# Linear attention, soft mixture of experts and an x − tanh(x) layer in one program: M is split into two parts while it is 128 columns wide, and the order of the last stage changes

## The chip, the cores and the metric

The program runs on one core of a Trainium2 chip. A core has TensorE (PE; its weight loads are shown apart, as PEld), VectorE (DVE), ScalarE (ACT), GpSimd (POOL) and SyncE (SP, which here only issues transfers). Each takes its instructions in a fixed order, written into the program beforehand. The metric is the device time of one execution in microseconds (us).

## What is computed

Three stages follow one another; the change is in the last, and in what hands over to it.

```python
# 1. attention with decay, in blocks: attn[4, 8, 768, 64] -> x[3072, 512]
# 2. soft mixture of experts
logits = x @ phi                                   # phi [512, 32]
d = softmax over tokens;  slot_input = d.T @ x     # 32 slots
h = np.maximum(slot_input[e] @ w1[e], 0.0)         # 8 experts
slot_out[e] = h @ w2[e]                            # [32, 512]
c = softmax(logits over the 32 slots)              # [3072, 32]
x = c @ slot_out
# 3. second layer, w_in [512, 2048], w_out [2048, 512]
h = x @ w_in
g = h - np.tanh(h)
out = g @ w_out
```

## The kernel before

**The last stage.** Since x = c @ slot_out, the product x @ w_in is c @ M with M = slot_out @ w_in, a matrix of only 32 rows and 2048 columns. The kernel never forms x: it makes M, and then h, 128 of its columns by 512 tokens at a time. For small h, h − tanh(h) is close to h³/3, and the kernel computes it as a mean part and a product: with d the deviation from the mean, r = (d + a) · (d²/3), where a comes from a table; what this leaves over is linear in c and is added at the end (the linear part, 32 columns wide). A check at the end of the program chooses a slower exact path, which these inputs do not take.

**Numbers in two parts.** A full-precision (fp32) product shows as two records on PE; a product of operands in the rounded form (fp32r) shows as one. To keep precision with rounded products, c stands in four slices of 32 rows of `c4` (rounded, rest, rounded, mean), and M stands in `ms` [128 rows, 2048 columns]: rows 0 to 63 the rounded M twice, rows 64 to 95 its rest.

**Chunks and turns.** The work is 96 chunks, numbered n. Chunk n is a pair (c, f): 512 tokens c and 128 columns f of h. `TURNS` lists the order: turns of 2, 2, 2, 4, 8, 12, 10 chunks and so on, each of one c; in the early turns only few f are there, since the weights still arrive. For a chunk, `d_of` forms d in one of three PSUM banks (0 to 2; L805), `s_of` squares it on ScalarE (L809), `r_of` multiplies on VectorE (L823; for seven chunks in `POOL_R` on GpSimd, L821), and `product` makes four products of 512 columns into banks 3 to 6 (L830, called t = 0 to 3 below). At a turn's end `keep` adds the four banks to `part` (ScalarE copies them when the turn begins at f = 0, L836; otherwise VectorE adds, L838), and the next turn reuses the banks. d runs three chunks ahead (`LA`), except for the chunks in `LATE`. In the last step of a turn the products of its last two chunks stand together, bank by bank.

**Weights.** w_in and w_out arrive as 64-bit numbers in slabs (`wi0`, `wo0`, `wi1`, ...), each by two transfers into a ring of three buffers, so that a slab's transfer waits until an earlier slab is used up. A slab is turned to fp32 by two `cast` steps on GpSimd (L117) and two `join` steps on VectorE (L121); `round_wo` rounds w_out (ScalarE L788, GpSimd L790). `DECODE_AT` and `LEAD` say at which chunk each step stands.

**M.** When two slabs of w_in are there, `make_m` forms 512 columns of M folded to 128 (four bands of 32 rows; L753, one PSUM bank called `MISC`), and a copy brings them to SBUF (L758). `put_m` spreads them out to `ms` through PSUM with the 0/1 matrix `put` (L765); ScalarE writes all 128 rows, rounding (L769), and VectorE then overwrites rows 64 to 95 with the difference (L770). `turn_m` makes a transposed copy for the table `mt` (L778, L781). The first 512 columns (m = 0) go in two halves, named (0, 0) and (0, 1) below; `HALF` and `DUE` say at which chunk. d of a chunk with f needs its columns of `ms`.

**The order** is written out by hand: a loop over n in which each call stands where its instructions go on every engine's queue, with `at(n, f)` for what is appended to step n:

```python
        if n + LA < NN and n + LA not in LATE:
            ahead()
        if n + LA - 1 < NN:
            r_of(n + LA - 1)
```

Matrix products on unused data (`keep_warm`, numbers in `WARM_MAIN`) stand in some waits.

## Time and profile before

| what | us |
|---|---|
| median of 3 runs (from 311.28 to 312.46) | 311.6 |
| the profiled execution, its own time | 311.51 |
| its span, from first to last instruction | 309.6 |
| PE busy, of the span | 294.8 |
| DVE busy | 181.3 |
| ACT busy | 134.3 |
| POOL busy | 115.2 |

The span is what the trace shows; 1.9 us lie around it. Times below are from the span's start. The last stage begins at about 155 us. The granted clock of TensorE is 0.995 of full speed over the span. Of two records in a row on PE the distance between starts counts, since products are pipelined: the length of one record holds the way through the array too.

### The profile page before, as it was taken

What the parts mean: (1) busy time and instruction counts of PE and PEld (TensorE: products, weight loads), DVE (VectorE), ACT (ScalarE), POOL (GpSimd) and SP (SyncE); (2) the same over time, 40 slices, a digit from 0 to 9 for tenths busy, and PEclk for the clock granted to TensorE, in tenths of its full rate; (3) what the DMA queues carried; (4) which work ended last, traced back from release to release, by engine and by line L of the source; (5) the groups of instructions that cost most, each with busy time, mean ns of one, the idle gap of its engine ahead of it and who ended that gap; (6) DMA issues with size and microseconds to landing.
All of it is one profiled execution on the core that took longest, in us unless ns stands there. A gap on an engine that the chain in (4) does not pass through costs nothing.

```text
span 309.6 us, 7420 instructions
## 1 busy us (share of the span) xinstructions
PE 294.8 (95%) x2996; PEld 213.6 (69%) x2996; DVE 181.3 (59%) x330; ACT 134.3 (43%) x280; POOL 115.2 (37%) x167
## 2 busy tenths in 40 slices
PE   8999999999999999999989889999999899999992
PEld 7788787878878774445466567777655677787771
DVE  4844455544654244520269667696872877968783
ACT  1433343344333433232248669586633554454420
POOL 6366566765653104112276445686600001000000
PEclk9999999999999999999999999999999999999997
DMA  6999999999999999999988747562000030303154
GB/s 209 386 402 395 396 399 394 395 399 398 392 403 396 383 362 344 389 393 396 391 308 318 268 142 285 194 230 110 0 2 0 2 135 0 135 2 135 70 202 143
DMA packets 32679, 79.77 MB, mean 258 GB/s; under 512 B 3008, under 2 KB 3328, under 8 KB 32640
## 3 DMA queue, kind: packets, MB, share of 16 engines
q1 hardware_dynamic: 32512, 79.18, 68.5%
q8 instruction: 25, 0.41, 0.5%
q14 instruction: 14, 0.11, 0.1%
q0 software_dynamic: 128, 0.07, 0.1%
HBM read 72.94 MB, written 6.29 MB: 256 GB/s over the span
## 4 chain that ended last, share of the span: by engine, by line
PE 80%; DVE 8%; issue 4%; DMA 3%; ACT 2%; POOL 1%; DVEq 0%; ACTq 0%; POOLq 0%
PE ops L830 22%; PE sc L286 7%; PE xp L310 7%; PE dps L805 6%; PE op L610 5%; PE hp L586 5%; PE xnp L344 4%; PE xp L303 4%; DVE r L823 3%; PE up L319 3%; DMA qk<-in_qkv 3%; DVE part L838 2%; PE ltp L333 2%; PE ap L388 2%; PE wp L419 2%
## 5 line engine op out<-in xcount | busy, mean ns | idle before, releaser
L830 PE MATMUL ops<-wr,r 128*128 128x512 f32 (+1 forms) x388 | 109.0, 397 | 1.2 <-ACT part L836 0.9
L830 PEld LDWEIGHTS ops<-wr,r 128*128 128x128 f32 x388 | 72.3, 188 | 22.2 <-ACT part L836 3.1
L809 ACT ACTIVATE s<-dps 128x512 f32<-128x512 f32 x96 | 56.9, 603 | 54.1 <-PE dps L805 52.8
L823 DVE SCALAR_TENSOR_TENSOR r<-dps,mt,s 128x512 fp32r<-128x512 f32 x89 | 64.8, 746 | 20.2 <-ACT s L809 19.4
L805 PE MATMUL dps<-c,ms 128*128 128x512 f32 x96 | 39.5, 425 | 4.2 <-DVE r L823 2.3
L290 DVE TENSOR_TENSOR at<-sc,dtab 128x512 f32<-128x512 f32 x48 | 30.8, 683 | 15.1 <-PE sc L286 15.1
L265 POOL TENSOR_TENSOR kc<-k,dtab 128x512 f32<-128x512 f32 x20 | 21.2, 1058 | 26.6 <-PE up L319 23.6
L258 POOL TENSOR_TENSOR qs<-qk,ql 128x512 f32<-128x512 f32 x20 | 25.5, 1275 | 14.6 <-DMA qk<-in_qkv 14.5
L346 ACT COPY xn<-xnp 128x512 f32<-128x512 f32 x24 | 14.0, 585 | 38.9 <-PE xnp L344 38.9
L286 PE MATMUL sc<-qk 64*128 64x128 f32 x384 | 27.9, 285 | 1.4 <-DMA qk<-in_qkv 1.4
L805 PEld LDWEIGHTS dps<-c,ms 128*128 128x128 f32 x96 | 17.9, 188 | 15.6 <-DVE r L823 7.8
L310 PE MATMUL xp<-at,v 128*64 128x128 f32 x384 | 26.3, 279 | 0.0
L286 PEld LDWEIGHTS sc<-qk 64*128 64x128 f32 x384 | 23.3, 187 | 4.2 <-issue 1.9
L313 ACT COPY xt<-xp 128x256 f32<-128x256 f32 x48 | 17.9, 372 | 16.9 <-PE xp L310 16.4
L310 PEld LDWEIGHTS xp<-at,v 128*64 128x64 f32 x384 | 20.5, 136 | 4.1 <-issue 3.9
L325 DVE TENSOR_TENSOR st<-up,sd 128x256 f32<-128x256 f32 x16 | 6.8, 425 | 23.4 <-PE up L319 22.0
L117 POOL CAST top<-wi 128x512 f16<-128x512 bf16 x16 | 14.3, 907 | 13.7 <-DMA wi<-in_w_in 13.1
L838 DVE TENSOR_TENSOR part<-ops,part 128x512 f32<-128x512 f32 (+1 forms) x29 | 17.9, 665 | 0.9 <-PE ops L1066 0.9
L610 PE MATMUL op<-w,hz 128*32 128x512 f32 x128 | 16.5, 594 | 0.0
L117 POOL CAST top<-wo 128x512 f16<-128x512 bf16 x16 | 15.2, 978 | 2.3 <-DMA wo<-in_w_out 2.1
L121 DVE SCALAR_TENSOR_TENSOR wif<-wi,top 128x512 uint32<-128x512 uint32 x16 | 13.3, 842 | 4.2 <-POOL top L117 4.2
L344 PE MATMUL xnp<-cst,xt 128*128 128x128 f32 x96 | 15.7, 287 | 0.0
(185 smaller groups left out, 344.3 us busy)
## 6 DMA issues: line engine op xcount, KB each, us to landing
w<-in_w SPq DMA_DIRECT2D x64, 512.0 KB, 8.4
qk<-in_qkv SPq DMA_DIRECT2D x24, 512.0 KB, 8.4
wi<-in_w_in SPq DMA_DIRECT2D x16, 512.0 KB, 4.0
wo<-in_w_out SPq DMA_DIRECT2D x16, 512.0 KB, 4.2
v<-in_qkv SPq DMA_DIRECT2D x24, 256.0 KB, 8.5
...
```

The lines of the kernel that those rows point to most:

```text
L117: nc.gpsimd.tensor_copy(out=every(top().bitcast(F16), 2, 1)[:, sl], in_=every(raw().bitcast(BF16)[:, 4:], 4, 0)[:, sl])
L258: nc.gpsimd.tensor_tensor(out=qs_t[u], in0=qk_t[u][:, 0], in1=ql, op=ALU.mult)
L286: nc.tensor.matmul(sc[h2][:, p], qk[sl, 1, p], qk[sl, 0, p], start=True, stop=True)
L290: nc.vector.tensor_tensor(out=by_head(at_t[u], h2), in0=sc[h2], in1=by_head(dtab, h2), op=ALU.mult)
L310: nc.tensor.matmul(at_head(p, h2), v[:, h * DH:(h + 1) * DH], at[:, h], start=c == 0 and p < 2, stop=True, skip_group_check=True)
L344: nc.tensor.transpose(xnp[:, p], xt[:, p // 2, p % 2], ident)
L610: nc.tensor.matmul(op[g * NS:(g + 1) * NS], hz_t[e % 3][:, q], w2_t[e, q // 4][:, g], start=e == 0 and q < 4, stop=e == NE - 1 and q >= 4, ...
L805: nc.tensor.matmul(d_t[n], ms[:, f * P:(f + 1) * P], c4[:, c], start=True, stop=True)
L809: nc.scalar.activation(out=s, in_=d_t[n], func=AF.Square, scale=math.sqrt(1.0 / 3))
L823: nc.vector.scalar_tensor_tensor(out=r_t[n], in0=d, scalar=mt[:, f, NS:], in1=s, op0=ALU.add, op1=ALU.mult)
L830: nc.tensor.matmul(op, r_t[n][:, t * P:(t + 1) * P], wr_t[f // 2][:, f % 2, sl], start=first, stop=last)
L838: nc.vector.tensor_tensor(out=pt, in0=op, in1=pt, op=ALU.add)
```

## The change

It makes six edits, all in what builds the instruction order.

1. `make_m` no longer only copies M: ScalarE writes the rounded M (`mh`) and VectorE the rest (`ml`), while M is 128 columns wide. `put_m` and `turn_m` use two rounded products each, one for `mh` and one for `ml`; `put` is 192 columns wide, so that `ml` lands on rows 64 to 95. The VectorE step on `ms` goes.
2. s and r of chunk 0 are made in two halves of 256 columns, and the products of chunk 0 stand ahead of d of chunk 3.
3. The two joins of `wi1`, which stood behind r of chunk 1, stand behind r of chunk 2 and of chunk 3.
4. The halves of m = 0 and the set m = 1 get places of their own (`HALF`, `SECOND`): `make_m(0, 1)` and `put_m(1)` stand in the middle of a turn's last products (`at_mid`), and `split` and `take` among the keeps. For all sets `put_m` now stands ahead of `turn_m`.
5. s of chunk 8 (`LATE`) stands behind the keeps of its step.
6. The linear part's end: one ScalarE copy, one VectorE difference and a ScalarE copy of 16 rows, in place of two ScalarE copies and four VectorE steps. The table `ends` goes. Two products of `keep_warm` go, one from each of two waits.

```diff
-WARM_MAIN = 2, 1, 2, 3, 1
+WARM_MAIN = 2, 1, 1, 2, 1
-HALF = 2, 3, 4
+HALF = 3, 4, 5
+SECOND = 7, 9, 9
...
+    mh, ml = (main.tile([P, P], F32R, name=n) for n in ("mh", "ml"))
...
-        m_t[m] = lt_all[:, DM + m % 2 * P:DM + (m % 2 + 1) * P]
-        (nc.vector.tensor_copy if half == 1 else nc.scalar.copy)(m_t[m][rows], mp_[rows])
+        def split():
+            nc.scalar.activation(out=mh[rows], in_=mp_[rows], func=AF.Copy)
+            nc.vector.tensor_tensor(
+                out=ml[rows], in0=mp_[rows], in1=mh[rows].bitcast(F32), op=ALU.subtract)
+        return split
...
         for j in js:
-            nc.tensor.matmul(
-                pp[:, j], put[rows, j], m_t[m][rows], start=True, stop=True, skip_group_check=True)
-        nc.scalar.activation(out=ms[:, sl], in_=pp, func=AF.Copy)
-        nc.vector.tensor_tensor(
-            out=ms[64:96, sl], in0=pp[64:96], in1=ms[64:96, sl].bitcast(F32), op=ALU.subtract)
+            for i, t in enumerate((mh, ml)):
+                nc.tensor.matmul(
+                    pp[:, j], put[rows, j, i * 64:i * 64 + P], t[rows], start=i == 0, stop=i == 1, skip_group_check=True)
+        def take():
+            nc.scalar.activation(
+                out=ms[:, m * 512 + js[0] * P:m * 512 + (js[-1] + 1) * P],
+                in_=pp[:, js[0]:js[-1] + 1].rearrange("p j f -> p (j f)"), func=AF.Copy)
...
-        nc.tensor.matmul(
-            tp.rearrange("p j s -> p (j s)"), m_t[m][rows],
-            tsel[rows, js[0]:js[-1] + 1].rearrange("p j s -> p (j s)"), start=True, stop=True)
+        for i, t in enumerate((mh, ml)):
+            nc.tensor.matmul(
+                tp.rearrange("p j s -> p (j s)"), t[rows],
+                tsel[rows, js[0]:js[-1] + 1].rearrange("p j s -> p (j s)"), start=i == 0, stop=i == 1)
...
+    pieces = lambda n: [slice(512)] if n else [slice(256), slice(256, 512)]
...
-            lambda: nc.vector.tensor_tensor(out=ql[96:], in0=qr[96:], in1=qh[96:], op=ALU.subtract),
-            lambda: nc.vector.tensor_scalar(
-                out=ql[96:], in0=ql[96:], scalar1=ends[96:, 1:2], scalar2=0.0, op0=ALU.mult, op1=ALU.add),
-            lambda: nc.vector.scalar_tensor_tensor(
-                out=qc[96:], in0=qh[96:], scalar=ends[96:, 0:1], in1=ql[96:], op0=ALU.mult, op1=ALU.add),
+            lambda: nc.scalar.activation(out=qc, in_=qr, func=AF.Copy),
             lambda: nc.vector.tensor_tensor(
-                out=qc[64:96], in0=qr[64:96], in1=qh[64:96], op=ALU.subtract),
+                out=qc[lo], in0=qr[lo], in1=qc[lo].bitcast(F32), op=ALU.subtract),
+            lambda: nc.scalar.activation(out=qc[96:112], in_=qr[96:112], func=AF.Copy),
...
-    now(early[1:])
+    cast_1, join_0, join_1, *early = early[1:]
+    now([cast_1] + early)
+    at_r(0, join_0)
+    at_r(1, join_1)
...
         if w == "wi" and i == 1:
-            at(HALF[0], lambda: make_m(0, 1))
-            at(HALF[1], lambda: turn_m(0, 1))
-            at(HALF[2], lambda: put_m(0, 1))
+            at_mid(HALF[0], lambda: make_m(0, 1))
+            at(HALF[1], lambda: put_m(0, 1)())
+            at(HALF[2], lambda: turn_m(0, 1))
+        elif w == "wi" and i == 3:
+            at(SECOND[0], lambda: make_m(1)())
+            at_mid(SECOND[1], lambda: put_m(1))
+            at(SECOND[2], lambda: turn_m(1))
         elif w == "wi" and i % 2:
-            at(n + DUE[0], lambda: make_m(i // 2))
-            at(n + DUE[1], lambda: turn_m(i // 2))
-            at(n + DUE[2], lambda: put_m(i // 2))
+            at(n + DUE[0], lambda: make_m(i // 2)())
+            at(n + DUE[1], lambda: put_m(i // 2)())
+            at(n + DUE[2], lambda: turn_m(i // 2))
...
-        if not last and (f + 2 != hi or n == 0):
+        if 0 < n and f + 2 < hi:
             for s in ops:
                 product(*s, n, f == lo, False)
         if last:
-            for s in ops:
+            take = None
+            for i, s in enumerate(ops):
+                if i == 2:
+                    take = run(n, due_mid)
...
             if n + LA in LATE:
-                ahead()
-            for s in ops:
+                d_of(n + LA)
+            for i, s in enumerate(ops):
+                if i == 2 and take:
+                    take()
                 keep(c, *s, lo, hi)
+            if n + LA in LATE:
+                s_of(n + LA)
```

**Where instructions stand, first place.** On PE, from the placing of the half (0, 0) of M to the products of the first turn, before (`pp` is put_m's, `tp` turn_m's, `wp` keep_warm's, `dps` d's, `ops` the products of a chunk, `mp` make_m's):

```order
L765 MATMUL pp<-lt_all,put 128x128 x2
L778 MATMUL tp<-tsel,lt_all 128x66
L624 MATMUL wp<-c_1932 128x512 x2
L805 MATMUL dps<-c_1932,ms 128x512 x3
L624 MATMUL wp<-c_1932 128x512 x3
L805 MATMUL dps<-c_1932,ms 128x512
L830 MATMUL ops<-wr_2332,r 128x512 x4
L805 MATMUL dps<-c_1932,ms 128x512
L830 MATMUL ops<-wr_2332,r 128x512 x4
L805 MATMUL dps<-c_1932,ms 128x512
L753 MATMUL mp__2509<-wif_2321,so 32x128 x8
```

and the same place on PE now:

```order
L776 MATMUL pp<-mh,put 128x128
L776 MATMUL pp<-ml,put 128x128
...
L791 MATMUL tp<-tsel,ml 128x66
L625 MATMUL wp<-c_1932 128x512
L818 MATMUL dps<-c_1932,ms 128x512 x3
L625 MATMUL wp<-c_1932 128x512 x2
L848 MATMUL ops<-wr_2336,r 128x512 x4
L818 MATMUL dps<-c_1932,ms 128x512 x2
L848 MATMUL ops<-wr_2336,r 128x512 x4
L818 MATMUL dps<-c_1932,ms 128x512 x2
L848 MATMUL ops<-wr_2336,r 128x512 x4
L760 MATMUL mp__2529<-wif_2325,so 32x128 x8
```

The four products of chunk 0 have moved ahead of d of chunk 3, and make_m of the half (0, 1) has moved from ahead of d of chunk 6 to the middle of the next turn's products.

**Second place.** On PE, from the end of make_m of the set m = 1 to d of chunk 14, before (turn 3 ends in the row `x8`):

```order
L753 MATMUL mp__2619<-wif_2321,so 32x128 x2
L805 MATMUL dps<-c_1932,ms 128x512
L830 MATMUL ops<-wr_2333,r 128x512 x8
L778 MATMUL tp<-tsel,lt_all 128x132
L805 MATMUL dps<-c_1932,ms 128x512
L830 MATMUL ops<-wr_2332,r 128x512 x4
L765 MATMUL pp<-lt_all,put 128x128 x4
L805 MATMUL dps<-c_1932,ms 128x512
```

and now:

```order
L760 MATMUL mp__2623<-wif_2325,so 32x128 x2
L818 MATMUL dps<-c_1932,ms 128x512 x2
L848 MATMUL ops<-wr_2337,r 128x512 x4
L776 MATMUL pp<-mh,put 128x128
L776 MATMUL pp<-ml,put 128x128
...
L848 MATMUL ops<-wr_2337,r 128x512 x4
L791 MATMUL tp<-tsel,mh 128x132
L791 MATMUL tp<-tsel,ml 128x132
L818 MATMUL dps<-c_1932,ms 128x512
L848 MATMUL ops<-wr_2336,r 128x512 x4
L818 MATMUL dps<-c_1932,ms 128x512
```

put_m has moved from directly ahead of d of chunk 14 to the middle of the last products of turn 3, ahead of d of chunk 13; and make_m stands one chunk earlier, ahead of the d of chunk 11 that it stood behind.

**Third place.** On DVE, the linear part's end among the r's (`e`, `qc`) and the keeps behind it (`part`), before:

```order
L823 SCALAR_TENSOR_TENSOR r<-dps,mt,s 128x512 x6
L897 TENSOR_TENSOR e<-qr,lt_all 32x512
L823 SCALAR_TENSOR_TENSOR r<-dps,mt,s 128x512
L898 TENSOR_SCALAR e<-e,ends 32x512
L823 SCALAR_TENSOR_TENSOR r<-dps,mt,s 128x512
L900 SCALAR_TENSOR_TENSOR qc<-lt_all,ends,e 32x512
L823 SCALAR_TENSOR_TENSOR r<-dps,mt,s 128x512
L902 TENSOR_TENSOR qc<-qr,lt_all 32x512
L823 SCALAR_TENSOR_TENSOR r<-dps,mt,s 128x512 x2
L838 TENSOR_TENSOR part_2343<-ops,part_2343 128x512 x4
```

and now:

```order
L888 TENSOR_TENSOR lt_all<-lt_all,g_2405 128x512
L840 SCALAR_TENSOR_TENSOR r<-dps,mt,s 128x512 x6
L913 TENSOR_TENSOR qc<-qr,qc 64x512
L840 SCALAR_TENSOR_TENSOR r<-dps,mt,s 128x512 x5
L856 TENSOR_TENSOR part_2347<-ops,part_2347 128x512 x4
```

Three of the four extra steps between the r's have gone from this queue.

## Rows read from the trace of the kernel before

**Rows 1.** The page: shares of the chain that ended last, by engine

```profile
PE 80%; DVE 8%; issue 4%; DMA 3%; ACT 2%; POOL 1%; DVEq 0%; ACTq 0%; POOLq 0%
```

**Rows 2.** Windows: stretch, its us, busy us per engine (instructions), PEclk, DMA

```profile
176.00:190.00 14.00, 12.53 (x82) 9.88 (x75) 9.66 (x17) 10.20 (x20) 6.74 (x8) 1.00 0.61 212
...
250.00:262.00 12.00, 12.00 (x55) 9.09 (x54) 8.43 (x18) 6.13 (x11) 1.05 (x5) 1.00 0.12 44
```

**Rows 3.** Timeline (start, us, engine, line): d of two neighbouring chunks, undisturbed

```profile
251.09 0.40 PE L805 MATMUL dps<-c,ms 128*128 128x512 f32 x1
...
252.26 0.39 PE L805 MATMUL dps<-c,ms 128*128 128x512 f32 x1
```

**Rows 4.** Timeline: the half (0, 0) of M, to the first r

```profile
156.38 0.26 ACT L758 COPY lt_all<-mp__2403 64x128 f32<-64x128 f32 x1 [1.17 <-PE mp__2403 L753]
...
156.69 0.71 PE L765 MATMUL pp<-lt_all,put 64*128 64x128 f32 x4 [0.36 <-ACT lt_all L758]
...
157.44 0.38 ACT L769 ACTIVATE ms<-pp 128x256 fp32r<-128x256 f32 x1 [0.80 <-PE pp L765]
...
157.85 0.42 DVE L770 TENSOR_TENSOR ms<-pp,ms 32x256 fp32r<-32x256 f32 x1 [1.99 <-ACT ms L769]
...
158.33 0.97 PE L805 MATMUL dps<-c,ms 128*128 128x512 f32 x3
...
158.87 1.57 ACT L809 ACTIVATE s<-dps 128x512 f32<-128x512 f32 x3 [1.04 <-PE dps L805]
...
159.50 1.41 DVE L823 SCALAR_TENSOR_TENSOR r<-dps,mt,s 128x512 fp32r<-128x512 f32 x2 [0.24 <-ACT s L809]
...
160.64 1.10 PE L830 MATMUL ops<-wr,r 128*128 128x512 f32 x4
```

**Rows 5.** Timeline: turns 0 to 3, joins, keeps, products and make_m

```profile
160.82 2.11 DVE L121 SCALAR_TENSOR_TENSOR wif<-wi,top 128x512 uint32<-128x512 uint32 x2
...
162.51 2.05 ACT L836 COPY part<-ops 128x512 f32<-128x512 f32 x4
...
164.17 0.68 DVE L121 SCALAR_TENSOR_TENSOR wf<-wo,top 128x512 uint32<-128x512 uint32 x1
...
165.41 2.02 PE L830 MATMUL ops<-wr,r 128*128 128x512 f32 x8
...
172.36 1.97 PE L830 MATMUL ops<-wr,r 128*128 128x512 f32 x4 [0.93 <-ACT part L836]
...
175.66 1.08 PE L753 MATMUL mp__2619<-wif,so 128*32 128x128 f32 x32
```

**Rows 6.** Timeline: put_m of m = 1 and d of chunk 14

```profile
180.28 1.05 PE L765 MATMUL pp<-lt_all,put 128*128 128x128 f32 x8
...
182.00 0.69 DVE L770 TENSOR_TENSOR ms<-pp,ms 32x512 fp32r<-32x512 f32 x1 [1.13 <-ACT ms L769]
...
182.74 0.50 PE L805 MATMUL dps<-c,ms 128*128 128x512 f32 x1 [1.41 <-DVE ms L770]
```

**Rows 7.** Timeline, POOL: the first cast of slab wi3

```profile
166.75 0.77 POOL L117 CAST top<-wi 128x512 f16<-128x512 bf16 x1 [1.27 <-DMA wi<-in_w_in]
```

**Rows 8.** Timeline: two later waits of PE

```profile
199.97 0.50 PE L805 MATMUL dps<-c,ms 128*128 128x512 f32 x1 [0.25 <-DVE ms L770]
...
221.36 0.50 PE L805 MATMUL dps<-c,ms 128*128 128x512 f32 x1 [0.45 <-DVE r L823]
```

**Rows 9.** Timeline: the linear part's end

```profile
242.15 0.48 DVE L898 TENSOR_SCALAR e<-e,ends 32x512 f32<-32x512 f32 x1
...
243.45 0.75 DVE L900 SCALAR_TENSOR_TENSOR qc<-lt_all,ends,e 32x512 fp32r<-32x512 f32 x1
...
245.04 0.50 PE L805 MATMUL dps<-c,ms 128*128 128x512 f32 x1 [0.79 <-DVE r L823]
```

**Rows 10.** Lines by form (busy us, mean ns), and one pair on the timeline

```profile
L830 PE MATMUL ops<-wr,r 128*128 128x256 f32 x8 | 1.7, 292 | 0.0
...
302.84 0.40 PE L830 MATMUL ops<-wr,r 128*128 128x256 f32 x2
```

More of the change, by code (lines that the diff above doesn't have):

```diff
@@ L741, in tile_main, with slices @@
     placed = set()
-    m_t = {}
+    mh, ml = (main.tile([P, P], F32R, name=n) for n in ("mh", "ml"))
+    def slices(half):
+        js = range(4) if half is None else range(2 * half, 2 * half + 2)
+        return js, slice(js[0] * NS, (js[-1] + 1) * NS)
     def make_m(m, half=None):
         mp_ = bank(MISC, [P, P], "mp_")
-        js = range(4) if half is None else range(2 * half, 2 * half + 2)
+        js, rows = slices(half)
         if half == 0:
@@ L760, in put_m @@
+        return split
     def put_m(m, half=None, bk=None):
         pp = bank(bk or MISC, [P, 4, P], "pp")
-        js = range(4) if half is None else range(2 * half, 2 * half + 2)
-        rows = slice(js[0] * NS, (js[-1] + 1) * NS)
+        js, rows = slices(half)
         for j in js:
-            nc.tensor.matmul(
-                pp[:, j], put[rows, j], m_t[m][rows], start=True, stop=True, skip_group_check=True)
-        pp = pp[:, js[0]:js[-1] + 1].rearrange("p j f -> p (j f)")
-        sl = slice(m * 512 + js[0] * P, m * 512 + (js[-1] + 1) * P)
@@ new lines, in take, with turn_m @@
+        def take():
+            nc.scalar.activation(
+                out=ms[:, m * 512 + js[0] * P:m * 512 + (js[-1] + 1) * P],
+                in_=pp[:, js[0]:js[-1] + 1].rearrange("p j f -> p (j f)"), func=AF.Copy)
+            placed.update(2 * m + j // 2 for j in js)
+        return take
+    def turn_m(m, half=None, bk=None):
+        js, rows = slices(half)
+        tp = bank(bk or MISC, [P, len(js), NS + 1], "tp")
+        for i, t in enumerate((mh, ml)):
+            nc.tensor.matmul(
+                tp.rearrange("p j s -> p (j s)"), t[rows],
+                tsel[rows, js[0]:js[-1] + 1].rearrange("p j s -> p (j s)"), start=i == 0, stop=i == 1)
@@ L822, in r_of @@
         else:
-            nc.vector.scalar_tensor_tensor(
-                out=r_t[n], in0=d, scalar=mt[:, f, NS:], in1=s, op0=ALU.add, op1=ALU.mult)
+            for sl in pieces(n):
+                nc.vector.scalar_tensor_tensor(
+                    out=r_t[n][:, sl], in0=d[:, sl], scalar=mt[:, f, NS:], in1=s[:, sl],
+                    op0=ALU.add, op1=ALU.mult)
     def product(op, t, sl, n, first, last):
@@ L974, in tile_main, with at_mid, at_r, run @@
     LA = 3
-    due = {}
+    due, due_mid, due_r = {}, {}, {}
     def at(n, f):
         due.setdefault(n, []).append(f)
-    def run(n):
+    def at_mid(n, f):
+        due_mid.setdefault(n, []).append(f)
+    def at_r(n, f):
+        due_r.setdefault(n, []).append(f)
+    def run(n, due=due):
+        then = None
         for f in due.pop(n, []):
-            f()
-    make_m(0, 0)
+            then = f()
+        return then
+    make_m(0, 0)()
     state = {}
@@ L989, in tile_main @@
     assert len(DECODE_AT) == len(parts)
-    put_m(0, 0, 3)
+    put_m(0, 0, 3)()
     turn_m(0, 0, 4)
@@ L1027, in decoded @@
                 at(LINEAR[1], lambda: state.update(linear=linear_3(state["qs"])))
-                for j in range(4):
-                    at(LINEAR[1] + 1 + j, lambda j=j: state["linear"][j]())
+                for j in range(3):
+                    at(LINEAR[1] + j, lambda j=j: state["linear"][j]())
                 at(CHECK[0], check_1)
@@ L1036, in tile_main @@
         last = f + 1 == hi
-        ahead = lambda: (d_of(n + LA), s_of(n + LA))
+        if f == lo:
+            ops = [(bank(3 + t, [P, DM], "ops"), t, slice(DM)) for t in range(B)]
+            if n + hi - lo == NN:
+                op = ops.pop()[0]
+                ops += [(op[:, :256], B - 1, slice(256)),
+                        (bank(MISC, [P, 256], "ops"), B - 1, slice(256, DM))]
+        if n == 0:
+            for s in ops:
+                product(*s, n, True, False)
         if n + LA < NN and n + LA not in LATE:
-            ahead()
+            d_of(n + LA)
+            s_of(n + LA)
         if n + LA - 1 < NN:
             r_of(n + LA - 1)
+        run(n, due_r)
         for slab, k in zip(parts, DECODE_AT):
@@ L1067, in tile_main @@
             if n + LA in LATE:
-                ahead()
-            for s in ops:
+                d_of(n + LA)
+            for i, s in enumerate(ops):
+                if i == 2 and take:
+                    take()
                 keep(c, *s, lo, hi)
+            if n + LA in LATE:
+                s_of(n + LA)
         run(n)
-    assert not due, sorted(due)
+    assert not due and not due_mid and not due_r
     scheduled.close()
```

41 lines of the change are left out of this document (10 added, 31 removed).

## The prediction

> **What bounds the kernel now.** I read the chain that ended last first: 80% of the span is PE, 8% DVE, 4% time in which an engine waited for nothing shown [rows 1]. So a shorter PE queue or a removed PE wait is worth its length, and other work counts only where PE waits for it. Then the windows. From 250 to 262 us PE is busy 12.00 of 12.00 and DVE 8.43: there nothing but PE counts, and a chunk takes what its five products of 512 columns take, 252.26 − 251.09 = 1.17 us, 0.233 each [rows 3]. From 176 to 190 PE is busy 12.53 of 14.00, and the granted clock is 1.00 (the 2.4 GHz level) in both [rows 2]: in the decoding stage, from the first M to about 226 us, PE waits at full clock. Timelines then say for whom: for the chain that makes `ms`, for r's that stand behind joins on DVE, and for keeps. The change works in that stage and at the linear part, so I lay the new order out by hand on the trace's durations, up to d of chunk 14, and take the later places one by one.
>
> **First half of M.** Before: copy 156.38, put 156.69, ScalarE's write 157.44, VectorE's difference 157.85, first d 158.33 [rows 4]. Now the difference comes first, 128 columns wide. It is not in the trace; VectorE's form takes 0.42 us at 256 columns and 0.69 at 512 [rows 4, 6], so 0.28 at 128 by the same slope (a bound from above is 0.42). Copy to 156.64, difference to 157.0. The first put product (for `mh`) goes at 156.69 as before; the second waits for `ml` until 157.05, the other two follow, and the last is through at 157.55. ScalarE's write of 0.38 ends at 157.96, with nothing behind it: first d at 158.0, 0.33 earlier. The difference stands on DVE ahead of the first w_out join; that join then ends near 157.75 and GpSimd's rounding of it at 158.4, while the first product needs it at 159.5: hidden, by one us. The put matrix costs GpSimd four more small copies at 118 us, far from the path.
>
> **A narrow rounded product.** Its price is the open one. The full-precision put takes (1.05 − 0.28)/7 = 0.11 a record, two records a product [rows 6]. The narrowest rounded product here has 256 columns: a pair takes 0.40, one alone 0.29, so 0.11 apart [rows 10]. At 128 columns it lies between half of that, 0.055, and the 0.22 of a full-precision product, if rounding saves nothing at this width. I take 0.11, the row nearest in kind. Then eight rounded products replace eight records at equal PE time, and two replace two in turn_m: no change.
> The Trainium skill (TensorE: Matmul & The Clock Gate, Back-to-back issue gap) gives about 81 ns per product for streams of weight loads and products 128 columns wide; by that, an estimate, a put would take 0.65 instead of 0.88 us and the sum would be some 0.9 us lower. No row before shows it.
>
> **Chunk 0 in halves.** s of 256 columns takes 0.38 (ScalarE's 256-column form), r 0.75 − 0.27 = 0.48 [rows 4]. From d at 158.0, with 0.54 until s starts as before: s halves end at 158.92 and 159.20, r halves at 159.45 and 159.88, and the products run from 159.5 and, the last two, 159.95 to 160.4. Before they ran from 160.64, behind d of chunk 3 [rows 4]. The halves cost ScalarE and VectorE some 0.2 us of queue each, which the next r, waiting for its s, hides.
>
> **Joins of wi1.** Before, both stood between r of chunks 1 and 2 and took 2.11 us; r of chunk 2 could only start at 162.9 [rows 5]. Now r of chunk 2 ends at 161.3, a join (0.68) and r of chunk 3 at 162.6, so d of chunks 5 and 6 go at 161.8 and 162.7. Turn 1's products then follow the keeps of turn 0 (four copies at 0.48 from 161.9, as in [rows 5]); make_m(0, 1), 1.0 us long, stands between them, and they end at 165.7. Before they ended at 165.41 + 2.02 − 0.17 = 167.3: 1.5 us ahead. Behind the second join, wi3's transfer waits for its buffer 0.4 us longer, its cast starts at 167.1 instead of 166.75 [rows 7]; its join is not due before 168.9.
>
> **The half (0, 1).** Its difference stands on DVE behind r of chunk 5 and a join of wi2, and ends at 166.9. Behind it, put_m holds PE: a new wait of 0.95 us, from 165.97. The lead stays at 1.5, since before the transpose, put and d stood there too. ms is ready at 168.35, d of chunk 8 asks for it at 169.2. s of chunk 8, moved behind the keeps, ends at 170.8 and delays its r to 171.6, which nothing asks for before 173. In return ScalarE's keeps come earlier: turn 3's first products go at 169.9 instead of 172.36, where they had waited 0.93 for a keep [rows 5]. Lead 2.4.
>
> **The set m = 1.** make_m at 172.0 instead of 175.66 [rows 5], lead 3.6, of which 1.2 is the chunk by which it moved. mh ends at 173.6, ml at 173.9; put starts at 174.4, between turn 3's products, without a wait. ScalarE writes ms at 176.25, between keeps. d of chunk 13 goes at 176.5, d of chunk 14 at 177.7. Before it went at 182.74, after 1.41 of waiting for VectorE's difference [rows 6]. **Lead 5.0** = 1.5 (joins and halves) + 0.9 (keeps) + 1.2 (make_m) + 1.4 (wait for ms).
>
> **Later.** The lead is kept if decoding keeps pace. The next slabs' transfers wait for joins, which are earlier by 0.5 (wi4), 2 (wi5) and 4 us (wo4), each with over 3 us to spare but wi5, which lands about as its cast is due. Four places remain. PE's wait for the difference at 199.97 [rows 8] goes, as put now stands a chunk ahead: 0.25 shown, 0.4 with the refilling of PE. At 221.36 PE waits 0.45 for an r that stood behind the difference and two joins [rows 8]; VectorE has 0.4 less work per set and no late wait there: 0.6 there, and 0.3 at the keeps that follow it. The linear part's four steps on DVE (two differences of 0.69 each, as a 512-column one takes, 0.48 and 0.75 [rows 6, 9]) become one of 0.69; with chunks of 1.17 and an r of 0.70, DVE has 0.47 spare a chunk, so one step no longer makes r late. PE's 0.79 wait at 245.04 [rows 9] goes, and the keeps behind it start earlier: 1.2. Sum 2.5, bounded by 0.8 (the linear wait alone) and 3.5. The two keep_warm products gone stood in waits: nothing.
>
> **Sum.** The profiled execution took 311.51 (median 311.6): 311.5 − 5.0 − 2.5 = **304.0 us**.
>
> **Rivals.** What this kernel's measurement can tell from no change is about 0.5%, 1.6 us.
> (a) *Narrow rounded products are as slow as full-precision ones*: 0.11 more for each of 40 (32 of put, 8 of turn_m): 4.4, so 308.4. For it: nothing here runs at 128 columns. Against: the 256-column pair shows no floor above 0.11.
> (b) *The lead is given back to decoding*: GpSimd's casts waited 1.27 for a transfer at 166.75 [rows 7]; if transfers or GpSimd's queue set the pace between 178 and 221, most of the 5.0 is waited away, and with 2.5 left the time is 309. Against: I found no cast waiting for a transfer after 175 us.
> (c) *The new difference blocks DVE*: it stands at once behind make_m in a fixed order, so r's behind it wait for make_m and ScalarE. If each of the sets 1 to 3 stops PE 0.8 us (one r and its start), 2.4 comes back: 306.4.
> (d) *The clock falls*, the slower case: with two warm products fewer, and new waits like the 0.95 at 166, the chip grants 1.2 GHz for a while. Each chunk at that level costs 1.17 more; from 6.4 chunks on (7.5/1.17) the change loses, and at twelve the time is 318. Against: before, the clock stood at 1.00 through a 1.41 wait [rows 2, 6].
> (e) *Nothing moves*: my layout misses a wait that holds the head as before, and only small gains stay: 311.
>
> **Chances.** Forecast 0.55 (its own range 302.3 to 306), (c) 0.08, (a) 0.19, (b) 0.11, of which half within 0.5%, (e) 0.02, (d) 0.05. Faster by over 0.5%: 0.55 + 0.08 + 0.19 + 0.05 = 0.87; within 0.5%: 0.06 + 0.02 = 0.08; slower: 0.05. The range reaches from 302.3 (later places at their upper bound, put a little faster) to 308.8 (case (a) and a little), which leaves out (b), (d), (e) and the edges.
>
> **What would show it.** First d at 158.0 behind ScalarE's write; chunk 0's products ahead of d of chunk 3 near 159.5; a PE wait of about 1 us ahead of put_m(0, 1); d of chunk 14 near 177.7, without a wait for DVE; no PE wait where the linear part ends, near 238; starts of put's products 0.11 apart. The prediction is wrong if those starts are 0.2 apart, if casts wait for transfers after 178, if the granted clock of a window in the last stage is under 1.00, or if d's wait for r's behind `ml`.

## The result, and the profile after

The changed kernel takes 307.04 us (median of 5, 306.54 to 308.24) where the kernel before took 311.6 (5 runs, 311.28 to 313.38): a ratio of 0.9857, 95% interval 0.9833 to 0.988, so 4.5 us faster. Forecast were 304.0 us and 7.5 us of gain. The profiled execution took 307.04, with a span of 305.3 (before: 309.6).

The page's chain that ended last, of the changed kernel, answers to [rows 1]:

```profile
PE 54%; DMA 33%; DVE 5%; issue 2%; SPq 1%; POOL 1%; ACT 1%; DVEq 0%; ACTq 0%; POOLq 0%
```

That is less PE and more DMA than before, but it is no new bound in the stage that changed. The DMA lines of the chain are `w`, `qk`, `v` and `k`, the inputs of attention and of the experts: another way back through the program's head, which the change leaves alone. The windows of [rows 2], now (stretch, its us, busy us and instructions of PE, PEld, DVE, ACT, POOL, then PEclk):

```profile
176.00:190.00 14.00, 13.08 (x60) 9.92 (x59) 12.35 (x17) 11.34 (x23) 9.37 (x9) 1.00 0.75 275
250.00:262.00 12.00, 11.89 (x54) 8.70 (x52) 9.81 (x23) 5.39 (x9) 1.06 (x5) 1.00 0.00 0
```

The granted clock stays at 1.00, the 2.4 GHz level. From 176 to 190 VectorE is now busy 12.35 of 14 us (9.66 before) and GpSimd 9.37 (6.74 before). VectorE's queue is nearly full there, and GpSimd's has no gap from 180.24 on, which matters below.

**A measure for what follows.** The spans differ by 4.3 us, but they mix the changed stage with two pieces that it does not touch. Timelines, PE, of the kernel before: the start of make_m(0, 0), and the last product:

```profile
155.26 0.96 PE L753 MATMUL mp__2403<-wif,so 128*32 128x128 f32 x14
...
303.44 0.28 PE L1066 MATMUL ops<-qc,c 128*128 128x256 f32 x1
```

The same two in the timelines of PE, VectorE and ScalarE of the changed kernel, with the way to the first products between them, which answers to [rows 4]:

```profile
156.07 1.07 PE L760 MATMUL mp__2408<-wif,so 128*32 128x128 f32 x16
157.49 0.28 DVE L766 TENSOR_TENSOR ml<-mp__2408,mh 64x128 fp32r<-64x128 f32 x1 [1.61 <-ACT mh L765]
157.51 0.32 PE L776 MATMUL pp<-mh,put 64*128 64x128 f32 x1 [0.37 <-ACT mh L765]
157.99 0.27 PE L776 MATMUL pp<-mh,put 64*128 64x128 f32 x1
158.10 0.27 PE L776 MATMUL pp<-ml,put 64*128 64x128 f32 x1
158.41 0.39 ACT L780 ACTIVATE ms<-pp 128x256 fp32r<-128x256 f32 x1 [0.95 <-PE pp L776]
158.85 0.96 PE L818 MATMUL dps<-c,ms 128*128 128x512 f32 x3
159.38 1.64 ACT L825 ACTIVATE s<-dps 128x256 f32<-128x256 f32 x4 [0.59 <-PE dps L818]
160.08 2.19 DVE L840 SCALAR_TENSOR_TENSOR r<-dps,mt,s 128x256 fp32r<-128x256 f32 x4 [0.49 <-ACT s L825]
160.71 1.16 PE L848 MATMUL ops<-wr,r 128*128 128x512 f32 x4 [0.43 <-DVE r L840]
...
298.72 0.28 PE L1095 MATMUL ops<-qc,c 128*128 128x256 f32 x1
```

I call the time from the first product of make_m(0, 0) to the start of the last product **PE's stretch**: 303.44 − 155.26 = 148.18 before, 298.72 − 156.07 = 142.65 after. The change gained **5.53 us** in it. The head, up to make_m, was 0.81 longer in this execution, and what lies behind the last product 0.42 longer (6.58 against 6.16): 5.53 − 0.81 − 0.42 = 4.3. All times "from make_m" below are counted from that first product of the same execution.

Where the lead stands, from make_m (before − after): first d 0.29; make_m(1) 20.40 − 17.86 = 2.54; d of chunk 14 27.48 − 23.57 = 3.91; d of chunk 21 36.05 − 33.45 = 2.60; d of chunk 26, where PE had waited 0.25 [rows 8], 3.06; first product of the linear part 73.73 − 69.87 = 3.86; the check's product behind it 105.39 − 99.99 = 5.40; last product 5.53. So two things ask for a reason besides the gains: 3.91 instead of 5.0 at d of chunk 14, and the loss of 1.31 right behind it. The loss shows on the timelines of PE and GpSimd:

```profile
178.44 0.45 PE L818 MATMUL dps<-c,ms 128*128 128x512 f32 x1
...
180.24 1.72 POOL L837 TENSOR_TENSOR r<-e,s 128x512 fp32r<-128x512 f32 x1 [4.74 <-ACT e L828]
181.89 1.94 POOL L118 CAST top<-wi 128x512 f16<-128x512 bf16 x2
183.75 1.04 POOL L803 CAST wr<-wf 128x512 fp32r<-128x512 f32 x1
184.85 1.20 PE L848 MATMUL ops<-wr,r 128*128 128x512 f32 x4 [0.18 <-POOL wr L803]
184.76 1.73 POOL L837 TENSOR_TENSOR r<-e,s 128x512 fp32r<-128x512 f32 x1
186.44 0.76 POOL L118 CAST top<-wi 128x512 f16<-128x512 bf16 x1
187.12 0.61 POOL L803 CAST wr<-wf 128x512 fp32r<-128x512 f32 x1
187.78 1.90 PE L848 MATMUL ops<-wr,r 128*128 128x512 f32 x7 [0.74 <-POOL wr L803]
```

The first row is d of chunk 13. From 180.24 GpSimd runs without a gap: r of chunk 13, two casts, a rounding of w_out, r of chunk 16, a cast, a rounding. PE waits for both roundings. Most of the lead at d of chunk 14 does not reach GpSimd: it was won between d of chunk 13 and d of chunk 14, where the kernel before waited. d of chunk 13 goes 22.37 from make_m (before 23.77), a lead of 1.40 only, and r of chunk 13 on GpSimd, which hangs on it, 24.17 (before 25.65). The two in the timelines of the kernel before:

```profile
179.03 0.48 PE L805 MATMUL dps<-c,ms 128*128 128x512 f32 x1
...
180.91 1.26 POOL L821 TENSOR_TENSOR r<-e,s 128x512 fp32r<-128x512 f32 x1 [6.02 <-ACT e L812]
```

### The profile page after: what moved, and what is told of

Read it like the earlier page. It is cut to its first block, busy times and chain, and to the rows that moved or that the text cites. A ratio compares the mean times of both kernels' runs of the same rounds, so it can differ in the third digit from the quotient of the medians.

```text
span 305.3 us, 7415 instructions
## 1 busy us (share of the span) xinstructions
PE 291.6 (96%) x2994; PEld 212.8 (70%) x2994; DVE 177.8 (58%) x327; ACT 134.2 (44%) x282; POOL 115.8 (38%) x168
## 4 chain that ended last, share of the span: by engine, by line
PE 54%; DMA 33%; DVE 5%; issue 2%; SPq 1%; POOL 1%; ACT 1%; DVEq 0%; ACTq 0%; POOLq 0%
PE ops L848 25%; DMA w<-in_w 17%; DMA qk<-in_qkv 8%; PE dps L818 7%; DMA v<-in_qkv 6%; PE op L611 5%; PE hp L587 4%; DMA k<-in_qkv 3%; DVE r L840 2%; PE ops L1095 2%; DVE part L856 1%; PE pp L776 1%; PE qp L900 1%; PE sc L287 1%; PE gp L682 1%
## 5 line engine op out<-in xcount | busy, mean ns | idle before, releaser
L825 ACT ACTIVATE s<-dps 128x512 f32<-128x512 f32 (+1 forms) x97 | 56.5, 599 | 46.9 <-PE dps L818 44.9
L840 DVE SCALAR_TENSOR_TENSOR r<-dps,mt,s 128x512 fp32r<-128x512 f32 (+1 forms) x90 | 65.1, 740 | 18.5 <-ACT s L825 17.8
L818 PE MATMUL dps<-c,ms 128*128 128x512 f32 x96 | 38.1, 416 | 0.2
L122 DVE SCALAR_TENSOR_TENSOR wif<-wi,top 128x512 uint32<-128x512 uint32 x16 | 14.0, 878 | 5.3 <-POOL top L118 5.3
L837 POOL TENSOR_TENSOR r<-e,s 128x512 fp32r<-128x512 f32 x7 | 10.3, 1478 | 13.8 <-ACT e L828 10.2
```

Of the source, the lines that this page charges most:

```text
L818: nc.tensor.matmul(d_t[n], ms[:, f * P:(f + 1) * P], c4[:, c], start=True, stop=True)
L825: nc.scalar.activation(out=s[:, sl], in_=d_t[n][:, sl], func=AF.Square, scale=math.sqrt(1.0 / 3))
L840: nc.vector.scalar_tensor_tensor(out=r_t[n][:, sl], in0=d[:, sl], scalar=mt[:, f, NS:], in1=s[:, sl], op0=ALU.add, op1=ALU.mult)
```

## The experiments

**Theories.** T1, my prediction's: the split of M removes the waits for VectorE's difference, the places and the late joins carry that lead forward, the linear end adds its own. Rivals: one part alone gives all of it; some parts give nothing; the lead is lost to decoding. All kernels in one table (median us; ratio to the kernel before as measured beside it, with its interval; start of make_m(0, 0) and of the last product in the profile; PE's stretch):

| kernel | median | ratio | make_m | last | stretch |
|---|---|---|---|---|---|
| before | 311.6 | 1 | 155.26 | 303.44 | 148.18 |
| changed | 307.04 | 0.9857 (0.9833–0.988) | 156.07 | 298.72 | 142.65 |
| e1, linear end alone | 310.0 | 0.9925 (0.9899–0.995) | 156.66 | 303.08 | 146.42 |
| e2, chunk 0 whole | 306.06 | 0.9812 (0.9779–0.9845) | 155.21 | 297.79 | 142.58 |
| e3, joins back | 306.67 | 0.9828 (0.9797–0.986) | 154.73 | 298.21 | 143.48 |
| e4, old places | 306.25 | 0.9817 (0.9772–0.9861) | 155.18 | 297.31 | 142.13 |
| e5, split alone | 310.02 | 0.995 (0.9931–0.9969) | 155.35 | 301.3 | 145.95 |
| e6, no split | 309.36 | 0.9936 (0.9913–0.996) | 155.13 | 301.04 | 145.91 |
| e7, r of 13 on VectorE | 305.03 | 0.9797 (0.9773–0.9821) | 154.92 | 296.67 | 141.75 |
| e8, own tile for s | 306.7 | 0.9845 (0.9818–0.9871) | 155.16 | 297.85 | 142.69 |
| e9, r of 15 on GpSimd | 306.27 | 0.9828 (0.9798–0.9859) | 154.76 | 297.13 | 142.37 |
| e10, e9 and chunk 0 whole | 306.16 | 0.982 (0.979–0.9849) | 157.15 | 299.6 | 142.45 |
| e11, r of 13 and 16 on VectorE | 305.24 | 0.9787 (0.9755–0.9819) | 155.34 | 296.78 | 141.44 |
| e12, changed, again | 306.0 | 0.9828 (0.9797–0.986) | 155.22 | 297.88 | 142.66 |

How to read it: make_m begins anywhere from 154.73 to 157.15, with no regard to the kernel. The intervals are 0.4 to 0.9% of the time wide, so that most parts cannot be told apart by the time. The stretch repeats to 0.01 us in e12, but that is one pair of executions. put_m(0, 1) goes 12.04 from make_m in e2 and 12.31 in e10, though their instructions up to there are the same, and 12.08 to 12.22 in the changed kernel, e7, e9, e11 and e12, which are the same up to there too. So differences of the stretch under 0.3 us decide nothing; larger ones carry the verdicts on parts.

**e12: the changed kernel again.** No edit.

> The changed kernel once more, unaltered. In its first profile make_m(0, 0) began at 156.07 us and in the kernel before at 155.26, with the program ahead of it the same up to GpSimd's few copies for the put matrix; in eight other profiles it began between 154.73 and 156.66. Theory 1 (that start is chance from one execution to the next, the rest is fixed): make_m(0, 0) at 154.7 to 156.7, stretch again 142.6 to 142.7, median 306.3 to 307.3. Rival (the change itself delays the head by 0.8): make_m(0, 0) at 155.9 to 156.3.

make_m at 155.22, stretch 142.66, median 306.0. So the late head of the first profile was chance, and theory 1 holds for the head and the stretch; the median lies 0.3 under its range. The two ratios' intervals overlap. The times expected of its variants below were counted from the first 307.04 and lie up to a microsecond high, so I compare stretches.

**e1: the linear part's end alone**, in the kernel before (the four steps on VectorE and `ends` go, and the new steps stand a chunk earlier):

```
+            lambda: nc.scalar.activation(out=qc, in_=qr, func=AF.Copy),
             lambda: nc.vector.tensor_tensor(
+                out=qc[lo], in0=qr[lo], in1=qc[lo].bitcast(F32), op=ALU.subtract),
+            lambda: nc.scalar.activation(out=qc[96:112], in_=qr[96:112], func=AF.Copy),
...
-                for j in range(4):
-                    at(LINEAR[1] + 1 + j, lambda j=j: state["linear"][j]())
+                for j in range(3):
+                    at(LINEAR[1] + j, lambda j=j: state["linear"][j]())
```

> The kernel before, with only the linear part's end in its new form (ScalarE writes qc, one VectorE difference, ScalarE writes 16 rows again). Theory: the four VectorE steps made the r's late, and PE's wait of 0.79 us near 245 goes; my term for it was 1.2 us, and between the two traces the lead grew from 3.05 at qr to 4.55 at the d that follows, so 1.5: 310.1 to 310.4 us, d of the waiting chunk without a PE wait. Rival: the lead that appears there belongs to the earlier changes (in the changed kernel VectorE enters that stretch with less behind it), and the new end alone gives 0.3 or less: 311.3 or more.

Stretch 146.42: 1.76 us of gain, above both my term and the theory's 1.5. On VectorE's timeline one step of 0.69 is left, and r's wait for ScalarE again:

```profile
241.35 0.69 DVE L895 TENSOR_TENSOR qc<-qr,qc 64x512 fp32r<-64x512 f32 x1 [0.95 <-ACT qc L894]
242.08 1.41 DVE L823 SCALAR_TENSOR_TENSOR r<-dps,mt,s 128x512 fp32r<-128x512 f32 x2
243.98 0.75 DVE L823 SCALAR_TENSOR_TENSOR r<-dps,mt,s 128x512 fp32r<-128x512 f32 x1 [0.49 <-ACT s L809]
```

PE's 0.79 wait of [rows 9] is gone, in this kernel as in the changed one. The waits ahead of it all stand (1.41, 0.25, 0.47), so this gain owes nothing to the other parts.

**e5: the split alone**, in the kernel before: `mh`, `ml`, the new `put`, `tsel`, put_m and turn_m; places, joins, keeps and the linear end as before.

> The kernel before with only the split of M (mh and ml, both placed by rounded products, ms ended by ScalarE), everything else at its place. I read it by PE's stretch, from the first product of make_m(0, 0) to the start of the last product: 148.18 us in the kernel before, 142.65 in the changed one, 146.42 with the linear end alone. Theory 1 (the split removes the waits for VectorE's difference: 0.3 at the first d, 1.41 at d of chunk 14 and 0.25 at the third set): stretch 146.2 to 146.6, gain 1.6 to 2.0, time 309.6 to 310.0. Rival (the waits only move, since the new difference stands in the queue between make_m and put): gain under 0.6, stretch over 147.6, time over 310.8.

Stretch 145.95, gain 2.23: more than the theory's 2.0. PE's waits, in two rows:

```profile
181.59 0.50 PE L816 MATMUL dps<-c,ms 128*128 128x512 f32 x1 [0.69 <-ACT ms L778]
242.89 0.50 PE L816 MATMUL dps<-c,ms 128*128 128x512 f32 x1 [0.79 <-DVE r L834]
```

The 1.41 for VectorE's difference [rows 6] became 0.69 for ScalarE's write; the waits of 0.25 and 0.45 [rows 8] are gone; the linear part's 0.79 stands. That the rest of the gain is VectorE's shorter queue is argued, not shown.

**e6: no split**, all else as in the changed kernel:

```
+            nc.tensor.matmul(
+                pp[:, j], put[rows, j], m_t[m][rows], start=True, stop=True, skip_group_check=True)
...
+            nc.vector.tensor_tensor(
+                out=ms[64:96, sl], in0=pv[64:96], in1=ms[64:96, sl].bitcast(F32), op=ALU.subtract)
```

> The changed kernel without the split: M whole, placed by full-precision products, ms ended by ScalarE and then VectorE's difference of 32 rows, all at the places of the changed kernel. PE's stretch is 142.65 us in the changed kernel. Theory 1 (the split is worth its terms wherever M is placed): 0.4 at the first d, and VectorE's difference late again behind put: stretch 143.6 to 144.6, time 308.0 to 309.0. Rival (the new places alone hide the difference, so the split is worth only the first d's 0.3 to 0.4): stretch 142.9 to 143.1, time 307.3 to 307.5.

Stretch 145.91: the split is worth 3.26 us in the changed kernel, above the theory's 1.0 to 2.0 and far above the rival's 0.25 to 0.45. New places without the split bring a wait that neither named:

```profile
188.15 0.50 PE L813 MATMUL dps<-c,ms 128*128 128x512 f32 x1 [1.72 <-DVE r L835]
184.64 2.79 DVE L122 SCALAR_TENSOR_TENSOR wif<-wi,top 128x512 uint32<-128x512 uint32 x2
187.35 1.40 DVE L835 SCALAR_TENSOR_TENSOR r<-dps,mt,s 128x512 fp32r<-128x512 f32 x2
```

Two joins on VectorE took 2.79 us together, and the r's behind them came late. VectorE's difference is late too, as theory 1 said: ahead of the transpose at 178.34 PE waits 0.48 for it.

**e4: old places**, with the split (make, transpose, put at the chunks of the kernel before):

```
-HALF = 3, 4, 5
-SECOND = 7, 9, 9
+HALF = 2, 3, 4
...
-            at(n + DUE[1], lambda: put_m(i // 2)())
-            at(n + DUE[2], lambda: turn_m(i // 2))
+            at(n + DUE[1], lambda: turn_m(i // 2))
+            at(n + DUE[2], lambda: put_m(i // 2)())
```

> The changed kernel with M split as in it, but make_m, turn_m and put_m of all sets but the first at the places of the kernel before (make, transpose, put, one chunk apart, set 1 a chunk later). Theory 1 (places and order carry the lead: 1.2 of my terms for the chunk by which make_m moved, and 0.4 + 0.6 later for put ahead of the transpose): 308.8 to 309.5, and d of chunk 14 waits on PE again. Rival (the split alone carries it, since ms now ends on ScalarE without a VectorE difference behind put): 307.0 to 307.6.

Stretch 142.13, **0.52 shorter** than the changed kernel's: T1 falls here. The new places do bring d of chunk 14 forward, to 23.57 from make_m instead of 24.19. But no PE wait for a rounding is left with the old ones. PE (d of chunk 13, then of chunk 14) and GpSimd:

```profile
176.46 0.45 PE L817 MATMUL dps<-c,ms 128*128 128x512 f32 x1
...
179.37 0.51 PE L817 MATMUL dps<-c,ms 128*128 128x512 f32 x1 [0.69 <-ACT ms L779]
178.32 1.63 POOL L836 TENSOR_TENSOR r<-e,s 128x512 fp32r<-128x512 f32 x1 [2.18 <-ACT e L827]
181.28 1.08 POOL L802 CAST wr<-wf 128x512 fp32r<-128x512 f32 x1
```

r of chunk 13 starts 23.14 from make_m there, and 24.17 in the changed kernel. PE's timelines say why: d of chunk 13 itself goes 21.28 from make_m there and 22.37 in the changed kernel, since the eight products of put_m (0.84) and one more d (0.23) now stand ahead of it. s of chunk 13 follows 0.54 to 0.55 behind its d in both, so ScalarE's write of `ms`, which stands between two pairs of keeps at the new place, adds nothing that shows. So the places that brought d of chunk 14 forward made d of chunk 13, and GpSimd's r behind it, a microsecond late.

**e7 and e11: r's taken from GpSimd.**

```
-POOL_R = 13, 16, 21, 26, 29, 34, 37
+POOL_R = 16, 21, 26, 29, 34, 37        # e7
+POOL_R = 21, 26, 29, 34, 37            # e11
```

> The changed kernel with r of chunk 13 on VectorE instead of GpSimd. In the changed kernel r of chunk 13 reaches GpSimd only at 180.24 (ScalarE wrote ms between the keeps first), and casts, roundings and r of chunk 16 queue behind it until PE waits 0.18 and 0.74 us for rounded w_out. Theory 1 (that queue gives back about 1 us of the lead): both waits go, stretch 141.6 to 141.9 against 142.65, time 306.0 to 306.3. Rival (VectorE has no room for one more r there, or the casts only wait for their transfers instead): 142.4 to 143.0, time 306.8 or more.

> The changed kernel with the r's of chunks 13 and 16 both on VectorE. Theory 1 (VectorE is full there: a join and an r take 1.34 to 1.42 us a chunk against 1.16 on PE, so it needs one r taken away): r's come late and PE waits for them, stretch 141.9 to 142.6. Rival (without GpSimd beside it VectorE's joins are short enough, and no r need go to GpSimd before chunk 21): 141.0 to 141.5.

e7: 141.75, both waits for roundings gone, and one of 0.64 for an r in their place. e11: 141.44, that wait down to 0.23. In e11 the rival was right: VectorE is not full there once GpSimd's r's are away. Lines by form, DVE, from 170 to 192 us (busy us, mean ns), of the changed kernel and then of e11:

```profile
L840 DVE SCALAR_TENSOR_TENSOR r<-dps,mt,s 128x512 fp32r<-128x512 f32 x12 | 8.8, 744 | 0.7 <-ACT s L825 0.6
L122 DVE SCALAR_TENSOR_TENSOR wif<-wi,top 128x512 uint32<-128x512 uint32 x6 | 6.0, 1004 | 0.6 <-POOL top L118 0.6
```

```profile
L840 DVE SCALAR_TENSOR_TENSOR r<-dps,mt,s 128x512 fp32r<-128x512 f32 x14 | 10.2, 741 | 0.6 <-ACT s L825 0.6
L122 DVE SCALAR_TENSOR_TENSOR wif<-wi,top 128x512 uint32<-128x512 uint32 x6 | 4.3, 723 | 0.0
```

Two r's more on VectorE cost it 1.4 us, and six joins of the same shape became 1.7 us shorter. The clearest single rows are of the same two joins of w_in. In e7 they take 2.38 together: 0.68 the first, which started ahead of r of chunk 16 on GpSimd, and 1.78 the second, from 182.75, beside it. In e11, with GpSimd idle, the first takes 0.68.

```profile
182.15 2.38 DVE L122 SCALAR_TENSOR_TENSOR wif<-wi,top 128x512 uint32<-128x512 uint32 x2
182.43 1.56 POOL L837 TENSOR_TENSOR r<-e,s 128x512 fp32r<-128x512 f32 x1 [1.64 <-ACT e L828]
185.25 0.50 PE L818 MATMUL dps<-c,ms 128*128 128x512 f32 x1 [0.64 <-DVE r L840]
```

```profile
182.64 0.68 DVE L122 SCALAR_TENSOR_TENSOR wif<-wi,top 128x512 uint32<-128x512 uint32 x1
183.34 0.78 POOL L118 CAST top<-wi 128x512 f16<-128x512 bf16 x1 [2.08 <-DVE wif L122]
185.32 0.51 PE L818 MATMUL dps<-c,ms 128*128 128x512 f32 x1 [0.23 <-DVE r L840]
```

This bears out a rule of the Trainium skill (SBUF — State Buffer, section "SBUF: two separate sides"): GpSimd and a VectorE instruction with two SBUF inputs share a pair of ports, as a lock for the whole instruction. The trace agrees: a join reads two SBUF tensors and goes from 0.68 to 1.78, ending 0.54 after GpSimd's r (183.99); VectorE's r reads PSUM and one SBUF tensor and stays at 0.74. Not only r's do it: in the changed kernel the join at 183.17 takes 1.15 beside a cast.

**e9: r of chunk 15 on GpSimd**, in place of 13 and 16.

```
-POOL_R = 13, 16, 21, 26, 29, 34, 37
+POOL_R = 15, 21, 26, 29, 34, 37
```

> The changed kernel with r of chunk 15 on GpSimd in place of those of chunks 13 and 16. With 13 moved to VectorE alone, PE's stretch (first product of make_m(0, 0) to start of the last product) was 141.75 us, with one wait left in this stage: 0.64 us at d of chunk 20, for r of chunk 17, which stood behind two joins in a row, since r of chunk 16 was not between them. Theory 1: r of chunk 16 back between the joins and 15 away from VectorE keeps both queues short: that wait goes, stretch 141.0 to 141.2. Rival: r of chunk 15 comes out of GpSimd after its products are due and PE waits there instead: 141.6 to 142.2.

Stretch 142.37 with a wait of 1.07 at d of chunk 20: worse than e7, and theory 1 fell. The wait is where it was, for r of chunk 17, so neither theory named its place rightly. With 15 away from VectorE, a join of w_out and one of w_in stand in a row ahead of r of chunk 16; the second takes 1.78 beside GpSimd's r (181.28 to 182.73), and the next one, ahead of r of chunk 17, 1.12 beside GpSimd's next steps:

```profile
181.49 1.78 DVE L122 SCALAR_TENSOR_TENSOR wif<-wi,top 128x512 uint32<-128x512 uint32 x1
```

At the new places each choice tried of early r's on GpSimd (13 and 16, 16 alone, 15) made joins longer.

**e2, e8, e10: chunk 0's halves.** e2 has chunk 0 whole, e10 is e9 with the same edit, and in e8 the first half of s goes to a tile of its own, which r's first half reads:

```
-    pieces = lambda n: [slice(512)] if n else [slice(256), slice(256, 512)]    # e2, e10
+    pieces = lambda n: [slice(512)]
...
+        s_first = tmp("e", bufs=2)[:, :256] if n == 0 else None    # e8
```

> The changed kernel with chunk 0 whole again (one s, one r of 512 columns). My prediction's step: halves let the first products go about 1 us earlier, and the head keeps some 0.5 of it. In the changed kernel's trace the first r half started only when both s halves were written, so the halves gain at most the difference of one whole r (0.75) and one r half (0.48), less their extra queue of 0.2. Theory 1 (halves are worth their predicted 0.5 to 1.0): 307.6 to 308.0. Theory 2 (the wait for both s halves takes it back): 307.0 to 307.3. Rival on the other side: halves cost, whole is faster by 0.2.

> The changed kernel, with the first half of chunk 0's s in a tile of its own, so that the first half of r needs only that one. In the changed kernel the first r half began at 160.08, 0.3 us after the first s half had ended, since it waited for both. Theory 1 (this wait is what the halves lost): first products 0.3 to 0.4 us earlier relative to make_m(0, 0), where PE waited 0.43, and the stretch 142.2 to 142.4 against 142.65. Rival (the lead there is lost again at the 0.78 us wait ahead of put_m(0, 1), as the run with chunk 0 whole ended no later): first products earlier, stretch unchanged, 142.5 to 142.8.

> The same, with chunk 0 whole. Chunk 0 whole alone changed the stretch from 142.65 to 142.58 us, since PE then waited 0.24 us less ahead of put_m(0, 1). Theory 1 (the halves' lead is always lost there): stretch within 0.1 us of the run with r of chunk 15 on GpSimd. Rival (that wait has gone, and the halves now count): 0.15 to 0.25 us longer than it.

e2: first products 4.84 from make_m instead of 4.64, but put_m(0, 1), where PE waits for `ml`, at 12.04 instead of 12.13: stretch 142.58. The halves gain 0.2 at the first products, and nothing of it shows at put_m(0, 1), which differs more between executions of one order. e10 against e9: 0.08 the other way. They are worth nothing that the stretch shows. In e8 not even the first products came earlier (4.63): with s in two tiles r's first half still began only when both halves of s were written.

```profile
158.46 0.38 ACT L826 ACTIVATE e<-dps 128x256 f32<-128x256 f32 x1 [0.58 <-PE dps L818]
158.75 1.36 ACT L826 ACTIVATE s<-dps 128x256 f32<-128x256 f32 x3
159.16 0.48 DVE L841 SCALAR_TENSOR_TENSOR r<-dps,mt,e 128x256 fp32r<-128x256 f32 x1 [0.48 <-ACT s L826]
```

The second s ends at 158.75 + 0.38 = 159.13, and r follows at 159.16. So the tile of s is not the reason. What is left in common is the bank of d, which both engines read. The Trainium skill (PSUM — Partial Sum Buffer, section "PSUM bank collisions raise a hardware error") says that two engines must not access one bank on the same partitions at once, reads included, so a program has to hold r back until ScalarE has done with the bank; by that, the rows agree. That d's halves in two banks would free r was not tried: it is argued, not shown.

**e3: the joins of wi1 back** ahead of r of chunk 2.

```
-    cast_1, join_0, join_1, *early = early[1:]
-    now([cast_1] + early)
-    at_r(0, join_0)
-    at_r(1, join_1)
+    now(early[1:])
```

> The changed kernel with the joins of wi1 back ahead of r of chunk 2, as in the kernel before. My prediction took the halves and the late joins together for a lead of 1.5 us at the end of turn 1. Theory 1: the joins are the larger part, r of chunk 2 starts 1.4 us later, PE waits for it in turn 0, and 1.0 to 1.4 us of the end time comes back: 308.0 to 308.4. Rival: PE then stands at put_m(0, 1) for the difference anyway (0.78 us of wait there in the changed kernel), so that up to 0.8 of it is hidden: 307.2 to 307.6.

Stretch 143.48: the late joins are worth 0.83, between the two expectations. PE waits 1.21 for an r, where the changed kernel waits 0.13, and the 0.78 ahead of put_m(0, 1) is gone:

```profile
163.15 0.50 PE L818 MATMUL dps<-c,ms 128*128 128x512 f32 x1 [1.21 <-DVE r L840]
...
167.67 0.32 PE L776 MATMUL pp<-mh,put 64*128 64x128 f32 x1
```

## Why the prediction came out as it did

The direction, the range and the mechanism of the split were right; the new places were not worth their terms (e4), and the time was 3 us too low. By PE's stretch, 7.5 forecast and 5.53 measured; the rest of the gap in the profile is the head and the tail (1.23), which vary with every execution.

- **First half of M.** Forecast 0.33 earlier, measured 0.29. `ml` took 0.28, as interpolated. Right.
- **Narrow rounded product.** I took 0.11 between starts; the rows at 157.99 and 158.10 show 0.11, and so do the starts of set 1's products from 176.50 to 177.16. The rival (a) is out. By the Trainium skill (TensorE: Matmul & The Clock Gate, Back-to-back issue gap) it would be about 81 ns; for these products the trace differs, and the measurement decides.
- **Chunk 0 in halves.** The step that failed here: "the products run from 159.5", 4.24 from make_m. They ran from 4.64, since r's first half waits for both of s, which the step left out. Of the 1.5 us given to halves and joins at turn 1's end, the joins bear 0.83 (e3) and the halves nothing (e2).
- **The half (0, 1).** The new wait came where forecast, 0.78 instead of 0.95:

```profile
168.20 0.32 PE L776 MATMUL pp<-mh,put 64*128 64x128 f32 x1 [0.78 <-DVE ml L766]
...
171.75 1.09 PE L848 MATMUL ops<-wr,r 128*128 128x512 f32 x4
...
173.93 1.08 PE L760 MATMUL mp__2623<-wif,so 128*32 128x128 f32 x32
179.64 0.39 PE L818 MATMUL dps<-c,ms 128*128 128x512 f32 x1
```

- **From there to turn 3.** I laid put_m(0, 1) to turn 3's first products out as 169.9 − 166.92 = 2.98; it took 171.75 − 168.20 = 3.55. The 0.57 is made of gaps of about 0.1 where PE goes between the 512-column products and the narrow ones of put_m and turn_m, and behind the first product after each, which I had set at nothing.
- **d of chunk 14.** Lead 5.0 forecast, 3.91 measured. Of the 1.09, 0.47 was missing at put_m(0, 1), laid out 11.66 from make_m and measured at 12.13, and 0.57 went in the gaps. PE stands at put_m(0, 1) for `ml`, and VectorE's queue has no idle time over 0.03 us from r's first half (160.08) to `ml`, so the 0.47 is VectorE's: its r's began 0.30 later than laid out, and a join at 164.09 took 1.20 instead of 0.68, beside a cast. d of chunk 14 waits for no difference, as forecast.
- **Rival (b), the lead given back to decoding.** It held in part. Its own sentence named "GpSimd's queue" between 178 and 221, and 1.31 was lost there, not most of the lead. I had argued against it from casts that wait for transfers, and looked at no other work in GpSimd's queue. e4, e7 and e11 show the cause: r's on GpSimd, later by a microsecond since put_m and a d stand ahead of d of chunk 13 at the new places, and longer joins beside them.
- **Later places.** Forecast 2.5. Measured from d of chunk 21 on: 5.53 − 2.60 = 2.93, of which the wait at 199.97 0.46 (0.4 forecast), the stretch to the linear part 0.80 (0.9), the linear part and the end 1.67 (1.2; 1.76 alone in e1). That the wait at 199.97 goes was forecast from put's new place; it is gone at the old places too (e4, e5), so the split alone does it. The term for the linear end was too small: one step instead of four, a chunk earlier, frees 2 us of VectorE's queue, and all of PE's wait goes with it.
- **Rivals (c) and (d).** `ml` stops PE only at put_m(0, 1), and the clock stood at 1.00 in both windows: neither came.

Together: 7.5 − 1.1 (head of the layout) − 1.3 (GpSimd) + 0.4 (later) = 5.5. Parts alone: split 2.23 (3.26 inside the changed kernel), linear end 1.76, together 3.99. The other 1.54 belongs to the joins (0.83 in e3) and to parts together: without the split all else brings 2.27 (e6), only 0.51 over the linear end alone. The halves bring nothing that shows (e2), and the places as they stand cost 0.52 (e4). s of chunk 8 and the two products of `keep_warm` were not tried alone. A version faster than both is e11, the change without two r's on GpSimd: 0.9787, with 141.44 of stretch against 142.66. Its interval of time overlaps with that of the changed kernel measured beside it; the stretch tells them apart by 1.22 us.

What stays open: whether old places and no early r's on GpSimd together would be faster still (not tried), and why r of a half waits for both s (argued only). Why put_m(0, 1) comes up to 0.27 apart in executions of one order, no run here tells.
